# DeltaNet and quick-GELU FFN on one core: raw keys with norms in row scales, and 32x32 transposes to the lanes, for chunks 0 and 1

## The chip, the core and the metric

The kernel runs on one core of a Trainium2 chip. The metric is the device time of one execution in microseconds. Engines: TensorE (PE, with PEld for its weight loads), VectorE (DVE), ScalarE (ACT), GpSimd (POOL) and SyncE (SP, which here only issues DMAs). Each has its own instruction stream; semaphores tie them together. DMAs are issued by SP, POOL or ACT.

## What is computed

A delta-rule recurrence for 4 batches of 8 heads, 768 steps, head width 48, and behind it a feed-forward block on the 3072 x 384 rows that result.

```python
k_n = k / (np.linalg.norm(k, axis=-1, keepdims=True) + 1e-06)
for t in range(S):
    y[:, :, t] = np.einsum('bhd,bhde->bhe', q[:, :, t], state)
    v_old = np.einsum('bhde,bhd->bhe', state, kt)
    state = state + bt[:, :, :, None] * np.einsum('bhd,bhe->bhde', kt, vt - v_old)
...
h = x @ w_in                                  # (3072, 384) @ (384, 2048)
g = h * (1.0 / (1.0 + np.exp(-1.702 * h)))
return (g @ w_out)                            # (2048, 384)
```

`q`, `k`, `v`, `beta` are float32. `w_in` and `w_out` reach the core as 64-bit words and are turned into float32 there by integer operations.

## The kernel before

**Tiling.** The 768 steps are cut into 6 chunks of 128. A *unit* is one chunk of one batch with its 8 heads; units are numbered chunk by chunk, `n = 4c + b`, so units 0 to 3 are chunk 0 and 4 to 7 chunk 1. In a chunk the recurrence becomes a triangular system: with G the Gram matrix of the keys, the updates U solve (I + diag(beta) strict_lower(G)) U = diag(beta) (V - K S). It is solved by blocks of 32 rows: the four 32x32 diagonal blocks of each head are inverted, and then come four steps of "multiply by the inverse of the block" (`solve`, PSUM tile `psU`, copied to `US` by ACT) and "subtract from the rows below" (`below`, tile `psR`, subtracted from `V` by DVE).

**The inverses.** Four units have 4 x 8 x 4 = 128 diagonal blocks, one for each SBUF partition ("lane"). Tile `NT` holds them with the 32x32 block along the free dimension, and `invert` works on all 128 lanes at once on DVE: multiply by beta (`NT<-NT,bI`), 15 growing products and sums for the 16-halves, 10 more for the corner, and a last multiply by beta (`NT<-YB,bI`). Blocks come to the lanes through DRAM (`Nd<-TW` or `Nd<-G`, then `NT<-Nd`) and go back through DRAM (`Yd<-NT`, then `XB<-Yd`). For chunks 2 to 5 `invert` works on two units at a time.

**Preparing a unit.** The keys are normalised in place (in chunk 0 by `normalize_first`, in chunk 1 by `normalize_mixed`, later by `normalize`, with POOL), transposed on PE (`turn`: `psT`, copied to `kT` by ACT), and `gram` makes G (`psG`, copied by ACT). `Step.scores` transposes the queries and makes the masked scores `M` (`psQ`; POOL's affine_select cuts the triangle). `queries`, `outputs` and `state` make the output (`psY`, copied to `xT` and `last`; `last` is spread over `xT` by six small DMAs for each pair of units) and the new state `ST`.

**Feed-forward.** `hidden` multiplies by `w_in` (`ph`, activation on ACT into tiles `gT`); `both_written`, `written` and, from the third pair on, `seven` (Strassen-like, with combinations of weights that POOL makes once in `combined`, tiles `TW` and `w_out`) multiply by `w_out` (`po`).

**Weights.** `fetch_in(i)` brings a quarter of raw `w_in` in 12 DMAs, 6 on SP and 6 on SP or POOL; raw words share space with `w_out`, two quarters at a time, so quarter 2 can come only when quarter 0 is converted. `conversion` takes five DVE operations and one on ACT for a piece; `fill(n)` emits n steps of that stream, so the code places them by hand between the other work. `fetches` names which DMA may follow which converted piece.

**Order.** Operations are pinned to program order, but for some of POOL and SP in `woven`. They run: load keys, normalise, blocks to the lanes, grams, `invert(0)` (with scores of units 0 to 3 on PE and ACT), hops of units 0 and 1 (`hops`, `together`: one unit solves while the other subtracts), `put_out`, hops of units 2 and 3 with `hidden` of the first pair and the keys of chunk 1 in between, `invert(1)` with `hidden` of both pairs, then the loop `woven`, in which three neighbouring units are in flight and a queue of feed-forward work is spent in shares. `warm(n)` puts n throw-away matmuls (`ps_warm`) on PE.

Of the kernel before, what the change touches and what calls it, by code (L numbers as in the profile page):

```python
# [18 lines left out]
def kernel(  # L19
# [39 lines left out]
    NW, NA, NY, NU = 80, 3, 28, 4  # L59
# [21 lines left out]
    QP += [TW[:, a : a + H * DP].rearrange("p (h d) -> p h d", h=H) for a in (2048, 2560)]  # L81
    NT = cpool.tile([128, BS, BS], F32, name="NT")
# [63 lines left out]
    act.activation(table, ident[:, 0:1], ACT.Copy)  # L146
# [21 lines left out]
    def quarter(i):  # L168
        size = KC * NQ * 2
        return as_raw(raws[:, i % 2 * size : (i % 2 + 1) * size], (KC, NQ))  # L170
# [13 lines left out]
    outside = {0: "xT", 8: "xT", 11: "xT", 1: "M", 9: "M", 14: "M", 2: "M2", 10: "M2", 15: "M2"}  # L184
    order = [0, 1, 2, 3, 4, 5, 6, 7, 8, 13, 9, 10, 12, 11, 14, 15]

    def fetch_out(f):

        if f in outside:
            slot = outside[f]  # L190
            if slot not in slots:
                slots[slot] = wk.tile([128, 2 * DM], I32, tag=slot[:2].strip("2"), name="raw", bufs=3)
            words = slots[slot]
        else:
            words = raws[:, inside[f] * DM : (inside[f] + 2) * DM]
        places[f] = as_raw(words, (1, DM))
        sync(out=as_rows(places[f])[:, 0], in_=moe_w_out[f * 128 : (f + 1) * 128, :])
# [51 lines left out]
    def conversions():  # L249
# [28 lines left out]
        ("in", 1): lambda: fetch_in(2),  # L278
        ("in", 3): lambda: fetch_in(3),
# [32 lines left out]
    def normalize_mixed(n):  # L312
        K = KN[n % len(KN)][:, :, 0:D]
        ksq = wk.tile([128, H, D], F32, tag="ksq", name="ksq", bufs=1)
        act.activation(ksq, K, ACT.Square)
        yield
        ssq = wk.tile([128, H], F32, tag="ssq", name="ssq", bufs=4)
        vec.tensor_reduce(ssq, ksq, axis=AX.X, op=ALU.add)
        rn = wk.tile([128, H], F32, tag="rn", name="rn", bufs=4)
        pool.tensor_tensor(rn, ssq, half, op=ALU.pow)  # L320
        yield
        vec.tensor_scalar(rn, rn, 1e-6, None, op0=ALU.add)
        vec.reciprocal(rn, rn)
        vec.tensor_tensor(K, K, rn.broadcast_to([128, H, D]), op=ALU.mult)
        yield

    def normalize_first():
# [3 lines left out]
        z = wk.tile([128, 4, B, H], F32, tag="ksq", name="z", bufs=1)  # L331
        x, y, t, s = (z[:, i] for i in range(4))
        sq = spare("squares")[:, 0 : 2 * H * D].rearrange("p (o h d) -> p o h d", o=2, h=H)
        for b in range(B):
            act.activation(sq[:, b % 2], KN[b][:, :, 0:D], ACT.Square)
            vec.tensor_reduce(s[:, b], sq[:, b % 2], axis=AX.X, op=add)
        ts(x, s, 1e-30, None, op0=ALU.max)
# [5 lines left out]
        tt(s, s, y, op=mult)  # L343
        ts(s, s, 1e-6, None, op0=add)
        vec.reciprocal(s, s)
        for b in range(B):
            K = KN[b][:, :, 0:D]
            tt(K, K, s[:, b].broadcast_to([128, H, D]), op=mult)
# [35 lines left out]
    def prepare(n):  # L384
# [4 lines left out]
        G = gram(n)  # L389
        Nd = dram.tile([H * NS], F32, tag="Nd", name="Nd", bufs=4)  # L390
# [8 lines left out]
            out=NT[b * NB * H : (b + 1) * NB * H],  # L399
# [7 lines left out]
    def spare(name):  # L407
        at = {"M": 0, "blocks": 0, "QS": 1024, "squares": 1024, "U": 2048, "M5": 2048}[name]
        return TW[:, at:]

    def diagonal(b, D_):

        kT = kTs[b]
        ps = [ps_seq.tile([128, NP, 128], F32, tag="seq", name="psD") for _ in range(2)]
        for h in range(H):
            r = slice(h % 2 * 64, h % 2 * 64 + D)
            pe.matmul(
                ps[h % 2][:, h // 2], lhsT=kT[r, h // 2, :], rhs=kT[r, h // 2, :],
                start=True, stop=True,
            )  # L420
        for e in range(2):
            for blk in range(NB):
                u = slice(blk * BS, (blk + 1) * BS)
                copy = vec.tensor_copy if e == 0 or blk == 0 else act.copy
                copy(D_[u, e::2, :], ps[e][u, :, u])

    def invert(c, b0=0, nb=B):
# [4 lines left out]
        bc = bI[part, c].broadcast_to([np, BS, BS])  # L432
# [34 lines left out]
        act.activation(X1, halves(Y)[1].rearrange("p l i -> p i l"), ACT.Copy)  # L467
# [20 lines left out]
        if c == 0:  # L488
            warm(NY, vec.memset)
        YS = N  # L490
        vec.tensor_tensor(YS, Y, bc, op=ALU.mult)
        if c == 0:
            gate = wk.tile([128, 1], F32, tag="gate", name="gate", bufs=1)
            pool.tensor_copy(gate, YS[:, 0, 0:1])
        dma = sync if c < 3 else nc.sync.dma_start
        groups = [range(b0, b0 + nb)] if c > 0 else [range(HB), range(HB, B)]
        back = {}
        for bs in groups:
            for b in bs:
                back[b] = dram.tile([H * C, BS], F32, tag="Yd", name="Yd", bufs=4)  # L500
                (beside if c == 0 and b >= HB else dma)(
                    out=back[b].rearrange("(p j) i -> p j i", j=BS),
                    in_=YS[(b - b0) * NB * H : (b - b0 + 1) * NB * H],
                )
            for b in bs:
                XB = wk.tile([128, H, BS], F32, tag="XB", name="XB", bufs=4)
                dma(out=XB, in_=back[b].rearrange("(h t) i -> t h i", h=H))
                inverse[c * B + b] = XB
# [8 lines left out]
    class Step:  # L517
# [19 lines left out]
        def scores(self):  # L537
# [7 lines left out]
            if c > 0:  # L545
# [4 lines left out]
                spare("M" if self.n < B else "M5")[:, 0 : H * 128].rearrange("p (h t) -> p h t", h=H)  # L550
                if self.n in (B - 1, B + 1)
# [121 lines left out]

    def g_tile():

        return wk.tile([128, FQ, NTH], F32, tag="gT", name="gT", bufs=GB)

    def hidden(xT, gT, t, cost, sums=None, late=False):

        n = t.stop - t.start  # L680
        for f0 in range(0, FC, 2):
            if f0 // FQ == len(gT):
# [43 lines left out]

# [85 lines left out]

    def both_written(c, gT):

        po = [ps_moe.tile([128, DM], F32, tag="moe", name="po") for _ in range(HB)]
        for n, f in enumerate(order):
            while ("out", f - f % 2 if 4 <= f < 8 else f) not in done:
                fill(1)
            fill(3)
# [64 lines left out]
    def follow(n):  # L884
# [6 lines left out]
        if n - 1 + B < len(units):  # L891
# [63 lines left out]
    for blk in range(NB):  # L955
        sync(out=bI[blk::NB, 0], in_=betas[:, 0, blk, :])
# [5 lines left out]
    fetch_in(0, other_queue)  # L962
# [3 lines left out]
    pool.memset(half, 0.5)  # L966
    pool.memset(ST, 0.0)
    for U in US:
        pool.memset(U[:, H * D :], 0.0)
    for i in range(B, len(KN)):  # L970
        pool.memset(KN[i][:, :, D:DP], 0.0)


    warm(NW)
    normalize_first()
    Ds = spare("blocks")[:, 0 : B * H * BS].rearrange("p (b h j) -> p b h j", b=B, j=BS)
    Nds = []
    turn(0)
    for b in range(B):
        if b + 1 < B:  # L980
            turn(b + 1)
        diagonal(b, Ds[:, b])
        Nd = dram.tile([H * C * BS], F32, tag="Nd", name="Nd", bufs=4)
        sync(out=Nd.rearrange("(h p k) -> p h k", p=C, k=BS), in_=Ds[:, b])
        Nds.append(Nd)
    for b in range(B):
        sync(
            out=NT[b * NB * H : (b + 1) * NB * H].rearrange("d i k -> d (i k)"),
            in_=Nds[b].rearrange("(d r) -> d r", r=BS * BS),
        )  # L990
    for b in range(B):
        load(b, ((QP, q),), sync)
    for b in range(B):
        load_values(b, sync)
# [150 lines left out]
```

## Time and profile before

| | us |
|---|---|
| three timed runs | 815.26, 820.82, 827.23 (median 820.82) |
| the profiled execution | 815.16 |
| its span, first to last instruction | 813.5 |
| busy: PE / weight loads / DVE / ACT / POOL | 748.9 / 636.4 / 501.4 / 238.5 / 249.4 |

The page cuts the span into 40 slices of 20.3 us; a digit is a busy share in tenths, PEclk the granted TensorE clock in tenths of full speed.

```profile
PE   8678889777789779999999999999999999999998
DVE  5797581998578667668767777786676681110000
PEclk9576599889799989999999999999999999999999
DMA  9945466244112410420421323224204102000000
```

From the fifteenth slice or so on PE is full and its clock is whole. In the slices ahead of that, some 290 us, PE is not full, the clock is often below one, and DVE is full in places. Some stages of that part, by the trace:

| us | what runs |
|---|---|
| 0 to 30.7 | keys, norms, blocks of chunk 0 to the lanes |
| 30.7 to 58.4 | `invert(0)` on DVE |
| 58.4 to 63.0 | inverses back, by DRAM |
| 63.0 to 87 | hops and outputs of units 0 and 1 |
| 87 to 125 | hops and outputs of units 2 and 3, keys of chunk 1, raw w_in converted |
| 125 to 142.5 | blocks of chunk 1 to the lanes, by DRAM |
| 142.5 to 171.2 | `invert(1)` on DVE |
| 171.2 to 220.3 | raw w_out converted, first steps of `woven` |
| 220.3 to 290.3 | `woven`, POOL's combinations of weights (267.3 to 282.0) |
| 290.3 to 813.5 | `woven` with both halves of its work, and the tail |

### The profile page before, as it was taken

Reading aid. Unit: us, or ns where it says so; the run is one execution under the profiler, and the core shown is the slowest. Engines: PE = TensorE matmul, PEld = TensorE weight load, DVE = VectorE, ACT = ScalarE, POOL = GpSimd, SP = SyncE. Lnnn points to the kernel's source line nnn. Section 1 sums busy time; section 2 is a strip of 40 time slices with the busy share of each in tenths; the row PEclk is TensorE's granted clock in tenths of the full one; section 3 lists DMA queues with packets and bytes.
Section 4 is the critical chain, followed back from the end, with each engine's and each line's share of the span. In section 5 each row is a group of like instructions: output and inputs, shape, how many; then the busy total and the mean of one; then the engine's idle time right before and its main releaser. Section 6 shows DMA issues by size and latency. Waiting matters only on the chain.

```text
span 813.5 us, 19675 instructions
## 1 busy us (share of the span) xinstructions
PE 748.9 (92%) x8464; PEld 636.4 (78%) x8464; DVE 501.4 (62%) x1029; ACT 238.5 (29%) x523; POOL 249.4 (31%) x210
## 2 busy tenths in 40 slices
PE   8678889777789779999999999999999999999998
PEld 6566668644456669889888898898898898998988
DVE  5797581998578667668767777786676681110000
ACT  3332263223323322242232232332422312312120
POOL 5011030011023826235254262282160330502213
PEclk9576599889799989999999999999999999999999
DMA  9945466244112410420421323224204102000000
GB/s 163 148 74 106 102 173 163 43 111 118 55 50 66 102 45 18 103 63 18 106 53 42 83 54 74 58 56 103 56 18 94 21 15 47 2 25 2 22 3 19
DMA packets 143654, 54.45 MB, mean 67 GB/s; under 512 B 113664, under 2 KB 138368, under 8 KB 143568
## 3 DMA queue, kind: packets, MB, share of 16 engines
q1 hardware_dynamic: 141936, 48.42, 27.0%
q0 software_dynamic: 1536, 4.52, 2.3%
q8 instruction: 66, 1.08, 0.6%
q10 hardware_dynamic: 96, 0.26, 0.1%
q14 instruction: 20, 0.16, 0.1%
HBM read 33.13 MB, written 18.87 MB: 64 GB/s over the span
## 4 chain that ended last, share of the span: by engine, by line
PE 70%; DVE 16%; DMA 4%; POOL 3%; issue 3%; SPq 2%; ACT 1%; DVEq 0%; POOLq 0%
PE ph L109 25%; PE po L109 24%; PE psY L109 6%; PE psU L109 5%; DVE P L109 4%; PE psQ L109 3%; DVE YB L109 3%; PE psT L109 2%; DVE TW L109 2%; PE psG L109 2%; SPq L109 2%; PE psR L109 2%; DVE NT L109 2%; DVE w_out L109 2%; POOL TW L711 1%
## 5 line engine op out<-in xcount | busy, mean ns | idle before, releaser
L109 PE MATMUL ph<-xT,w_in 128*128 128x256 f32 x1152 | 268.7, 390 | 0.0
L109 PEld LDWEIGHTS ph<-xT,w_in 128*128 128x128 f32 x1152 | 219.8, 194 | 33.3 <-DVE V L109 1.4
L109 PE MATMUL po<-w_out,gT 128*128 128x192 f32 (+1 forms) x736 | 152.8, 361 | 18.7 <-DVE w_out L109 11.0
L109 PEld LDWEIGHTS po<-w_out,gT 128*128 128x128 f32 x736 | 122.3, 193 | 37.2 <-DVE w_out L109 14.8
L711 POOL TENSOR_TENSOR gT<-gT 128x512 f32<-128x512 f32 x80 | 105.8, 1331 | 124.6 <-ACT gT L109 114.1
L109 DVE TENSOR_TENSOR V<-V,psR 64x384 f32<-64x384 f32 (+1 forms) x96 | 53.3, 556 | 134.7 <-PE psR L109 133.5
L109 DVE TENSOR_TENSOR P<-NT,YB 64x2 f32<-64x2 f32 (+9 forms) x200 | 98.4, 492 | 6.4
L109 ACT ACTIVATE gT<-ph 128x512 f32<-128x512 f32 x92 | 54.9, 596 | 152.9 <-PE ph L109 152.8
L109 PEld LDWEIGHTS psU<-V,XB 32*32 32x32 f32 x1536 | 61.6, 109 | 31.5 <-issue 16.5
L109 DVE TENSOR_REDUCE YB<-P 64x2 f32<-64x2 f32 (+9 forms) x200 | 81.8, 409 | 6.9
L109 PE MATMUL po<-TW,gT 128*128 128x192 f32 x480 | 83.0, 328 | 0.0
L109 ACT COPY US<-psU 32x384 f32<-32x384 f32 x92 | 43.2, 469 | 125.0 <-PE psR L109 115.4
L109 PE MATMUL psU<-V,XB 32*32 32x48 f32 x1536 | 73.0, 209 | 6.5 <-DVE V L109 4.8
L109 PEld LDWEIGHTS po<-TW,gT 128*128 128x128 f32 x480 | 77.9, 190 | 1.1 <-issue 0.3
L109 PE MATMUL psR<-US,G 32*32 32x48 f32 x2208 | 63.1, 207 | 0.6 <-ACT US L109 0.5
L578 POOL TENSOR_SCALAR_AFFINE_SELECT M<-M 128x1024 f32<-128x1024 f32 x19 | 23.6, 1245 | 123.5 <-DVE M L109 62.1
L109 DVE TENSOR_TENSOR o<-o,po 128x192 f32<-128x192 f32 x40 | 13.5, 351 | 75.8 <-PE po L109 75.3
L109 PEld LDWEIGHTS psR<-US,G 32*32 32x32 f32 x2208 | 53.5, 108 | 2.0 <-ACT US L109 1.1
L94 POOL DMA_DIRECT2D KN<-in_k_dram x15 | 14.4, 959 | 99.0 <-PE psY L109 99.0
L109 DVE TENSOR_TENSOR P<-NT 64x512 f32<-64x512 f32 (+7 forms) x50 | 43.0, 860 | 2.1
L109 PE MATMUL ps_warm<-ident 128*128 128x256 bf16 x176 | 31.5, 339 | 11.4 <-ACT G L109 6.5
L109 PE MATMUL psQ<-QS,kT 48*128 48x176 f32 (+1 forms) x368 | 35.5, 337 | 4.9 <-ACT QS L109 4.8
(110 smaller groups left out, 776.8 us busy)
## 6 DMA issues: line engine op xcount, KB each, us to landing
Nd<-G SPq DMA_DIRECT2D x20, 512.0 KB, 3.5
V<-in_v_dram SPq DMA_DIRECT2D x24, 192.0 KB, 3.2
out_dram<-o SPq DMA_DIRECT2D x24, 192.0 KB, 2.6
QP<-in_q_dram SPq DMA_DIRECT2D x22, 192.0 KB, 3.4
w_out<-in_moe_w_in_dram SPq DMA_DIRECT2D x18, 192.0 KB, 4.6
raw<-in_moe_w_out_dram SPq DMA_DIRECT2D x9, 384.0 KB, 4.0
NT<-Nd SPq DMA_DIRECT2D x24, 128.0 KB, 2.6
XB<-Yd SPq DMA_DIRECT2D x24, 128.0 KB, 3.1
```

The costliest lines, as they stand in the source:

```text
L94: dma(out=place(dst, n)[:, :, 0:D], in_=src[b, :, c * C : (c + 1) * C, :].rearrange("h p d -> p h d"),)
L109: return lambda *a, **kw: tc.keep_in_program_order(op(*a, **kw))
L578: (pool if self.n < B else nc.gpsimd).affine_select(out=self.M, in_=self.M, compare_op=ALU.is_gt, fill=0.0, base=0, pattern=[[0, H], [1, 1 ...
L711: (engine or nc.gpsimd).tensor_tensor(o, a, b, op=op)
```

## The change

- Keys of chunks 0 and 1 are no longer scaled. They are transposed and multiplied raw. With l the length of a key, the system is solved for U/l: `lengths` makes l, turns it to the lanes by a 32x32 transpose (`across`) and puts beta / l^2 (`scale`) in place of beta in `invert`; `lengthen` multiplies the values by l. `normalize_first` and `normalize_mixed` go.
- Diagonal blocks of these chunks are made by 32x32 matmuls of their own (`diagonal`), two units in a pair of PSUM banks, copied by two operations, and go to the lanes and back by DVE transposes of 128x1024 (`lanes`, `tokens`). The DRAM trips of these two chunks go; chunks 2 to 5 keep theirs.
- The four units of chunk 0 hop in one loop, two pairs in turn; their outputs follow one after the other. The first pair's `hidden` and chunk 1's keys come behind that.
- Raw quarters 0 and 1 of `w_in` lie in `GT`, the space of the `gT` tiles, so that all four are fetched at the start; queries and values are loaded earlier too. `w_out` pieces 2, 10 and 15 come through `TW`.
- Warm matmuls are fewer: 80 to 14 at the start, 36 around the grams and scores of chunk 0 to none, 28 to 12 (and not held for DVE) before the hops, 4 to 2 in each hop. The activation table of the GELU is loaded at the start.
- 18 steps of w_out's conversion are put ahead of `invert(1)`, and `both_written` begins within it as far as pieces are converted.

```diff
-    NW, NA, NY, NU = 80, 3, 28, 4
+    NW, NA, NY, NU, NF = 14, 3, 12, 2, 18
...
+    def squares(n, sq):
+        act.activation(sq, KN[n % len(KN)][:, :, 0:D], ACT.Square)
+        vec.tensor_reduce(
+            sums_of[:, n % B * H : (n % B + 1) * H], sq, axis=AX.X, op=ALU.add
+        )
+
+    def lengths(c):
...
+        tt(length, sums_of, y, op=mult)
+        ts(length, length, 1e-6, None, op0=add)
+        vec.transpose(across, length)
+        vec.reciprocal(scale, across)
+        tt(scale, scale, scale, op=mult)
+        tt(scale, scale, bI[:, c], op=mult)
+
+    def lengthen(n):
+        V = loaded[n]
+        vec.tensor_tensor(
+            V, V, length[:, n % B * H : (n % B + 1) * H].broadcast_to([128, H, D]), op=ALU.mult
+        )
...
+    def lanes():
+        vec.transpose(
+            NT.rearrange("p i k -> p (i k)"), Ds.rearrange("p l k -> p k l")
+        )
+
+    def tokens(c):
+        vec.transpose(
+            XBs.rearrange("p l i -> p i l"), NT.rearrange("p j i -> p i j")
+        )
...
-        bc = bI[part, c].broadcast_to([np, BS, BS])
+        bc = (bI[part, c] if c > 1 else scale).broadcast_to([np, BS, BS])
...
-        act.activation(X1, halves(Y)[1].rearrange("p l i -> p i l"), ACT.Copy)
+        (vec.tensor_copy if c < 2 else act.copy)(X1, halves(Y)[1].rearrange("p l i -> p i l"))
...
+    warm(NW)
+    for n in range(B):
+        squares(n, sq[:, n % 2])
+        turn(n)
+        diagonal(n)
+        if n == 1:
+            keep_diagonals(n)
+    lengths(0)
+    keep_diagonals(B - 1)
+    lanes()
...
+    warm(NY)
...
+    paths = hops(*pair[:2]), hops(*pair[2:])
     for i in range(2 * NB):
-        together(*next(path))
-        warm(NU)
-        fill(1)
-    for s in pair[:2]:
+        for path in paths:
+            together(*next(path))
+            warm(NU)
+            fill(1)
+        if i % 2:
+            pair[i // 2].select()
+    for s in pair:
         put_out(s)
-        fill(1)
+        fill(2)
...
     while not ("in", 7) in done:
-        fill(1)
+        ahead_of(preparing, 1)
+        fill(2)
+        feed()
     run(preparing)
+    fill(NF)
+    both = both_written(0, gTs[0])
+    for n in range(B, 2 * B):
+        lengthen(n)
     inverting = invert(1)
     first = new_step(B)
-    for i in range(25):
+    for i in range(27):
         ahead_of(inverting, 1)
         feed()
+        if not ffn and i % 2:
+            next(both)
```

## The prediction

> **What bounds it now.** I read the page's slices first, then the windows cut at the stages of the program, then the chain that ended last, then VectorE's timeline at the places where that chain changes engine. The windows (us from the span's start; busy us of PE, weight loads, DVE, ACT, POOL; granted clock; DMA share; GB/s) say where PE is the limit and where not:
>
> ```profile
> 0.00:30.70 30.70, 23.08 (x191) 18.83 (x193) 18.13 (x53) 11.89 (x26) 10.98 (x33) 0.83 0.87 150
> 30.70:58.40 27.70, 21.24 (x161) 16.45 (x158) 25.83 (x54) 11.18 (x27) 0.00 (x0) 0.68 0.71 98
> ...
> 63.00:87.00 24.00, 22.16 (x434) 17.43 (x434) 15.84 (x22) 7.29 (x18) 1.49 (x1) 0.64 0.40 82
> ...
> 125.00:142.50 17.50, 17.50 (x93) 15.14 (x92) 1.57 (x2) 4.98 (x10) 0.55 (x1) 1.00 0.63 167
> 142.50:171.20 28.70, 22.42 (x99) 18.63 (x97) 26.87 (x57) 6.54 (x14) 1.09 (x1) 0.88 0.17 30
> 171.20:220.30 49.10, 35.86 (x311) 21.17 (x312) 40.80 (x84) 15.47 (x29) 8.64 (x7) 0.87 0.42 111
> ...
> 290.30:813.50 523.20, 515.80 (x5961) 462.02 (x5959) 288.43 (x603) 142.03 (x318) 182.04 (x139) 1.00 0.20 47
> ```
>
> From 290 us on, TensorE is busy 515.8 of 523.2 us at full clock. The instruction order there is unchanged, so I carry these 523.2 us over. All that the change can win lies before, where VectorE (25.8 of 27.7 us, 26.9 of 28.7, 40.8 of 49.1) and the DMA carry the chain:
>
> ```profile
> 24.61 2.14 DMA Nd<-TW
> 26.77 0.30 SPq L109
> 27.12 3.57 DMA QP<-in_q_dram
> 30.69 1.22 DVE NT L109
> ...
> 57.21 1.20 DVE NT L109
> 58.47 2.02 DMA Yd<-NT
> ```
> ```profile
> 132.35 7.60 DMA Nd<-G
> 139.97 2.56 DMA NT<-Nd
> 142.54 1.24 DVE NT L109
> ```
>
> The reader should see the two trips through DRAM: blocks to lanes (24.6 to 30.7 in chunk 0, 132.4 to 142.5 in chunk 1) and back (58.4 to 63.0, the first psU). Before chunk 1's solve VectorE stands:
>
> ```profile
> 142.54 1.23 DVE L109 TENSOR_TENSOR NT<-NT,bI 128x1024 f32<-128x1024 f32 x1 [15.94 <-DMA NT<-Nd]
> ```
>
> **Start to the first solve.** Before: norms, four key scalings (1.96 us), the psT/psD chain, 32 partial copies, two DMA legs; the solve starts at 30.7. After: keys are transposed raw as they land (ACT takes them at 3.87, 5.17, 6.45, 7.93). Per unit ACT has one square (0.52) and one kT copy (0.60), and psT takes 0.67. The last kT is out near 10.0, psD (0.7, as a 16-instruction psU group at full clock) near 10.8. VectorE's norm chain took 9.07 to 11.98; with a small transpose and two multiplies at 0.2 each and the reciprocal (0.35) it runs from 10.0 to 13.9, then one psD copy (0.5) and a 128x1024 transpose. No row shows a transpose: bounds are 0.9 (1024 elements at the rate of the fastest 768-element row, 0.69) and 4.46 (a 1024-element multiply, NT<-NT,bI at 274.2, stretched beside POOL); I take 1.25, because the nearest row is the undisturbed 1024-element multiply, 1.22. Solve starts at 15.7: 15.0 us won. Beta, now on the path, is queued just behind the keys on SP and has some 6 us of slack.
>
> **First solve to the first hop.** Same instructions, 27.7 us, plus the X1 copy on VectorE (0.42, a 128x256 copy), two value scalings (0.56 each) and the transpose back (1.25): 30.5, so the first psU is at 46.2 instead of 63.0. The lead is now 16.8. Grams, scores and selects of four units (8x0.55 + 4x0.60 + 16x0.3 = 11.6 us of ACT) hide under the solve. Queries and values are loaded earlier: SP issues four keys (2.73), four betas (2.88), four queries (3.35), six pieces of w_in (4.45) and then the values, near 14 to 20; by bytes keys 0.8, queries 0.8, first w_in quarter 1.6 and values 0.8 MB at the slices' 150 GB/s are in at 27 us, before the 42 where values are scaled. All four raw quarters and three more keys make 9.2 MB, 61 us; the last quarter is converted after 90. So the early w_in costs nothing; without that cover it would cost what the trace shows at 102 us, where VectorE stands 5.09 us for raw w_in, a stall that goes. Queued behind 24 POOL issues (0.54 each, six took 3.23) is now the memset of the late U, and ACT's fourth US copy waits for that: the last issue waits for the 16th piece to land, 2.1 MB, which at half of 150 GB/s takes 28 us from 7, so 35, against 47 when needed. At a quarter of the rate it would be 63: bounds 0 and 16 us; I take 0, by the two queues' equal shares of w_in.
>
> **Hops of four units.** 16 groups alternate between two pairs. VectorE needs 16 subtractions at 0.56 and 16 conversion steps, about 14 of 0.9 us of them waiting for nothing: 21.4. A group on PE at half clock is 16 steps at 0.079 plus two warm matmuls (0.97/2): 1.8 to 1.85, so 29.6; at full clock VectorE's 21.4 binds. PE idles some 20 us before, as the 12 warms are no longer held for the solve's end. I take 27, to 73.
>
> The clock, row first: granted 0.50 from 24 us; though PE was fed from 28.5, it came back to 1.00 only near 46, and it fell to 0.5 again from 68 to 84 while small matmuls ran. The Trainium skill (TensorE: Matmul & The Clock Gate, part 1) speaks against cutting warms: an idle window of about 3.4 us halves the clock, but by it one busy window restores it. By the rule the hops would take about 23 us and the total would be 4 lower; the row shows a slower return, so the row decides.
>
> **Put-outs, keys of chunk 1.** Four put-outs of 16+16 psY at half clock (4.68 a pair): 9.4, to 82. The change adds a wait: `last` is one buffer, so ACT's copy for the third unit waits for six xT DMAs (SP issue 4.6, landing 1.8). Queued behind it on ACT are a conversion step and the next square, for which VectorE waits: 89 before it goes on, 6 of them idle. Then 16 w_in steps (0.9) and reduces, with ACT per unit 3.7 us (square, kT, two G, relu, gelu): 18 us, to 107. Then norms 3.9, two psD copies, two steps and the transpose: 114.6. The G round trip (10.1 us and 15.9 of idle VectorE) is gone. Next are 18 w_out steps (0.48): 123, and four value scalings: 125.5. Second solve: 28.7 + 0.4 + 1.25, to 155.7 against 171.2. DMA in that stretch: keys 0.8, queries 0.4, values 0.8 and eight raw pieces of w_out at 0.39, 5.1 MB from 76 on at the 158 to 226 GB/s of the windows; raw w_out lands some 5 us ahead of its conversion.
>
> **After the second solve.** 52 of the 70 w_out steps are left against 69; 17 x 0.5 = 8.5 us shorter, since this stretch is VectorE's (40.8 of 49.1 busy): 40.6. Then 47.0 as before. The four POOL combinations (3.45+3.43+3.40+4.30, then psT after 7.86 us of idle PE) come one po group earlier in POOL's order; the key scaling behind the first waits 3.4, the rest leave earlier: gain 0 to 6, I take 4.
>
> **Sum.** 16.8 + 0.2 (46.2 to 125.5 against 63.0 to 142.5) - 1.5 + 8.5 + 4 = 28 us. The profiled execution took 815.2 (813.5 plus 1.7 around it): 787. It was the fastest of those shown; the median is 5.7 above. Halfway, I predict 790.
>
> **Rivals.** (1) VectorE alone binds between first psU and second solve: its work there is 9.0 + 36 + 1.4 + 2.2 + 3.9 + 2.2 + 8.6 + 2.3 = 66 instead of my 79, gain 41, so 774 profiled and about 777. For it: full clock in hops and SP early enough with xT. Against: 0.5 clock in both old hop stretches. (2) The tail of the prologue does not shorten: conversions still wait for raw w_out, which now shares the DMA with keys, queries and values, and POOL's combinations stall as before. Then 28 - 8.5 - 4 = 15.5 remain: 800, about 803. For it: 226 GB/s at 172 to 180, a full queue. Transposes at the upper bound (4 x 3.2 = 13) land there too. (3) The clock stays at half until the second solve's end: after psD at 114, 69 hidden matmuls remain (two passes of 0.22 each, 30.3), psT and psQ 2, po 6.5: 38.8 against 41 until the solve is over. So it begins to cost below a mean clock of 0.95. At 0.5 it costs 36 here, 3 in the hops and 8 in the key loop (psT, two ph groups, psG: 3.1 a unit becomes 6.1, 24.6 for four against 18, and psD): 47 - 28 = 19 slower, 834, about 837. The gain is gone where 38.8 grows by 17 beside the other 11, at a mean clock of 0.7. Against: dense hidden matmuls had 1.00 from 112 to 156. (4) The change doesn't do what it says: a wait on beta, values or the late U puts the solve or hops back by 6 to 10: 795 to 798.
>
> **Chances.** Forecast 0.53 (own range 781 to 798), rival 1 0.18, rival 2 0.19, rival 3 0.05, rival 4 0.05. The range takes in rival 1 down to 772 and rival 2 to 808. Two per cent, about what a measurement here tells from no change, is 804.4: faster 0.53 + 0.18 + 0.05 + 0.09 of rival 2 = 0.85; same 0.11 with the rest of rival 2 and a milder rival 3; slower 0.04.
>
> **What would show it.** NT's first multiply near 16 us with no DMA before it; first psU near 46; clock near 0.5 in the hops; some 6 us of idle VectorE at the third put-out; the second NT multiply near 125 with no DMA wait; psT after the combinations near 261. I am wrong if a transpose takes over 3 us, if ACT or PE ends the wait before V in chunk 1, or if the part from that psT on is not 523 us long.

## The result, and the profile after

The changed kernel took 813.73 us (median of 19 runs, 810.43 to 815.83); the kernel before took 820.44 in the same job (19 runs, 811.83 to 827.23). The ratio is 0.9935, 95% interval 0.9915 to 0.9955: 0.65% faster, where 3.7% was forecast, and outside the range. The profiled execution of the changed kernel spans 812.0 us, so its own time is at the median; the one of before, with 813.5 us, was among the fastest of its kernel. The two traces therefore differ by 1.5 us where the medians differ by 6.7: where the other 5 us of the kernel before arise, no trace here shows.

The windows of the changed kernel, cut at its own stages (us from the start; busy us of PE, weight loads, DVE, ACT, POOL; granted clock; DMA share; GB/s):

```profile
0.00:20.50 20.50, 11.78 (x305) 9.18 (x306) 9.01 (x28) 6.81 (x14) 14.03 (x39) 0.82 1.10 155
20.50:53.40 32.90, 21.90 (x140) 17.84 (x139) 31.06 (x57) 12.11 (x28) 7.46 (x11) 0.50 1.08 180
53.40:84.90 31.50, 31.50 (x672) 23.14 (x672) 23.57 (x34) 11.09 (x20) 0.00 (x0) 0.50 0.07 12
84.90:99.50 14.60, 10.78 (x139) 9.32 (x138) 7.65 (x13) 5.21 (x17) 1.83 (x2) 0.73 0.29 63
99.50:124.80 25.30, 23.01 (x383) 18.65 (x384) 20.68 (x41) 12.56 (x24) 0.83 (x1) 0.89 0.69 174
124.80:136.50 11.70, 4.16 (x19) 3.31 (x18) 11.46 (x23) 3.75 (x6) 0.00 (x0) 0.83 0.36 108
136.50:174.00 37.50, 33.35 (x152) 27.04 (x150) 29.52 (x60) 7.95 (x16) 1.09 (x1) 0.96 0.03 6
```

The rows are: start, first solve, hops, put-outs, key loop, w_out steps, second solve. The trips through DRAM are gone: the first multiply on NT waits for no DMA any more (its line is below, at 136.55). But in the hops TensorE is busy all the time (31.50 of 31.50 us), in the w_out steps TensorE works 4.16 of 11.70 us, and in the second solve it works 33.35 of 37.50 where it had 22.42 of 28.70 before.

Where the lead arises and where it ends is read from the timelines of the engines. "Solve" is the first multiply on NT, "psQ n" the first score matmul of unit n; e1 to e18 are the experiments below.

| kernel | solve 1 | first psU | solve 2 | psQ 6 | psQ 7 | psQ 8 | psQ 9 | median us |
|---|---|---|---|---|---|---|---|---|
| before | 30.7 | 63.0 | 142.5 | 225.6 | 247.6 | 267.2 | 307.6 | 820.4 |
| changed | 20.5 | 53.4 | 136.6 | 224.4 | 247.9 | 274.2 | 305.8 | 813.7 |
| forecast | 15.7 | 46.2 | 125.5 | | | | | 790 |
| e1 | 20.9 | 53.7 | 128.9 | 218.0 | 241.6 | 264.4 | 304.4 | 811.7 |
| e2 | 20.9 | 53.7 | 142.3 | 227.5 | 251.1 | 277.4 | 309.4 | 817.6 |
| e3 | 20.3 | 53.1 | 134.6 | 212.6 | 235.0 | 261.0 | 292.9 | 801.5 |
| e4 | 20.4 | 53.2 | 135.4 | 223.9 | 247.3 | 273.6 | 305.2 | 813.0 |
| e5 | 20.5 | 53.4 | 134.5 | 222.6 | 246.1 | 272.4 | 304.0 | 813.4 |
| e6 | 20.2 | 58.5 | 139.9 | 227.4 | 250.8 | 277.1 | 310.6 | 821.0 |
| e7 | 17.0 | 52.1 | 134.8 | 222.4 | 245.9 | 272.2 | 303.8 | 813.0 |
| e9 | 20.4 | 53.2 | 130.4 | 218.4 | 245.1 | 271.3 | 303.0 | 811.5 |
| e10 | 21.0 | 53.8 | 136.4 | 224.2 | 247.6 | 268.8 | 301.7 | 819.9 |
| e11 | 20.9 | 53.8 | 137.1 | 225.2 | 248.6 | 269.8 | 306.3 | 814.1 |
| e12 | 18.7 | 53.9 | 130.9 | 218.3 | 245.0 | 271.1 | 302.9 | 806.5 |
| e13 | 20.4 | 53.3 | 128.1 | 215.6 | 237.0 | 263.6 | 296.1 | 805.1 |
| e14 | 17.8 | 51.3 | 127.3 | 216.0 | 239.7 | 266.1 | 297.6 | 802.9 |
| e15 | 18.0 | 50.4 | 124.7 | 213.4 | 235.0 | 261.6 | 294.1 | 801.7 |
| e17 | 20.6 | 53.5 | 136.4 | 224.1 | 245.5 | 272.1 | 304.6 | 812.4 |
| e18 | 29.6 | 62.2 | 144.8 | 227.4 | 248.8 | 268.5 | 305.4 | 809.5 |

A lead of 10.2 us at the first solve is 9.6 at the first psU, 6.0 at the second solve, 1.2 at psQ 6 and 1.8 at psQ 9; from there to the end both kernels need the same (506.1 and 505.9 us). e5 has the changed kernel's instructions in the same order (why is told below), and its second solve came 2.0 earlier: differences of 2 us between two profiles mean nothing, and the medians decide.

The lines that answer to the wait on NT of before are, on PE and then on DVE:

```profile
135.80 4.57 PE L111 MATMUL ph<-xT,w_in 128*128 128x256 f32 x12 [7.54 <-ACT GT L111]
```
```profile
136.55 1.22 DVE L111 TENSOR_TENSOR NT<-NT,small 128x1024 f32<-128x1024 f32 x1
...
159.77 0.42 DVE L111 TENSOR_TENSOR V<-V,psQ 128x96 f32<-128x96 f32 x2 [6.05 <-PE psQ L111]
```

VectorE no longer stands 15.94 us before the second solve. But during that wait TensorE had been busy 17.50 of 17.50 us with the hidden layer, which now lies elsewhere: when the second solve began, 115 of its 192 matmul records had started before the change, and 74 after it. What is left runs inside the solve, and V waits 6.05 us for psQ, which stands behind it.

### The profile page after: what moved, and what is told of

It reads as the page before. It is cut to its first block, busy times and chain, and to the rows that moved or that the text cites. A ratio compares the mean times of both kernels' runs of the same rounds, so it can differ in the third digit from the quotient of the medians.

```text
span 812.0 us, 20270 instructions
## 1 busy us (share of the span) xinstructions
PE 747.4 (92%) x8794; PEld 633.9 (78%) x8794; DVE 505.5 (62%) x1030; ACT 234.5 (29%) x512; POOL 245.9 (30%) x217
## 3 DMA queue, kind: packets, MB, share of 16 engines
q8 instruction: 69, 1.13, 0.6%
## 4 chain that ended last, share of the span: by engine, by line
PE 78%; DVE 15%; issue 3%; ACT 2%; DMA 1%; POOL 0%; SPq 0%; DVEq 0%; POOLq 0%; ACTq 0%
PE ph L111 30%; PE po L111 25%; PE psU L111 7%; PE psY L111 5%; DVE P L111 4%; PE psQ L111 4%; DVE YB L111 2%; PE psT L111 2%; PE psR L111 2%; DVE NT L111 2%; PE psG L111 2%; DVE w_out L111 2%; PE ps_warm L111 1%; DMA xT<-last 1%; DVE TW L111 1%
## 5 line engine op out<-in xcount | busy, mean ns | idle before, releaser
L111 PE MATMUL po<-w_out,GT 128*128 128x192 f32 (+1 forms) x736 | 155.4, 365 | 16.1 <-DVE w_out L111 12.4
L111 PEld LDWEIGHTS po<-w_out,GT 128*128 128x128 f32 x736 | 123.9, 195 | 36.0 <-DVE w_out L111 16.5
L736 POOL TENSOR_TENSOR GT<-GT 128x512 f32<-128x512 f32 x80 | 105.9, 1332 | 122.8 <-ACT GT L111 112.2
L111 DVE TENSOR_TENSOR V<-V,psR 64x384 f32<-64x384 f32 (+1 forms) x96 | 53.3, 556 | 138.9 <-PE psR L111 137.7
L111 ACT ACTIVATE GT<-ph 128x512 f32<-128x512 f32 x92 | 54.8, 596 | 153.5 <-PE ph L111 153.4
L111 PEld LDWEIGHTS psU<-V,XB 32*32 32x32 f32 x1536 | 67.6, 116 | 39.4 <-issue 31.4
L111 PE MATMUL psU<-V,XB 32*32 32x48 f32 x1536 | 79.1, 217 | 11.0 <-DVE XB L111 11.0
L111 PE MATMUL po<-TW,GT 128*128 128x192 f32 x480 | 83.0, 328 | 0.0
L111 PEld LDWEIGHTS po<-TW,GT 128*128 128x128 f32 x480 | 77.9, 190 | 1.1 <-issue 0.3
L111 DVE TENSOR_TENSOR P<-NT 64x512 f32<-64x512 f32 (+7 forms) x50 | 48.8, 976 | 1.9
L308 POOL TENSOR_TENSOR rn<-ssq,half 128x8 f32<-128x8 f32 x16 | 35.0, 2186 | 12.8 <-DVE ssq L111 12.8
```

The costliest lines, as they stand in the source:

```text
L111: return lambda *a, **kw: tc.keep_in_program_order(op(*a, **kw))
L308: nc.gpsimd.tensor_tensor(rn, ssq, half, op=ALU.pow)
L736: (engine or nc.gpsimd).tensor_tensor(o, a, b, op=op)
```

## The experiments

Unless another is named, an edit is to the changed kernel. Times are medians, compared with the kernel before on the same chip.

**The w_out steps and the hidden layer.**

e1:
```diff
-    NW, NA, NY, NU, NF = 14, 3, 12, 2, 18
+    NW, NA, NY, NU, NF = 14, 3, 12, 2, 0
```


> None of the 18 w_out steps is put ahead of the second solve; they follow it. Theory A (the lead is lost because the GELUs of the hidden layer stand behind these steps on ScalarE, so that TensorE waits 7.5 us and VectorE later 6.0 us at V): the second solve starts 8 us earlier, near 128, TensorE has no wait of over 2 us before it, the hidden layer is done before V needs psQ, and of the 8.7 us of steps put behind the solve some hide under the po matmuls; total 806 to 810. Theory B (VectorE binds from the put-outs to the fifth group and the steps cost the same wherever they stand): the start is 8 us earlier, the stretch after the solve 8.7 us longer, total 812 to 816.

e2:
```diff
-    fill(NF)
+    for _ in range(NF):
+        fill(1)
+        feed()
```


> The 18 w_out steps stay ahead of the second solve, but a step of the hidden layer is issued after each. Theory A (order on ScalarE): TensorE's 7.5 us at GT goes, the hidden layer is done some 15 us earlier, VectorE's 6.0 us at V goes and the first po matmuls run beside the solve; total 6 to 8 us less than the changed kernel, 805 to 808. Theory B (VectorE binds): the waits go but TensorE stands later at w_out instead; total 811 to 814.

e3:
```diff
-                for j in range(KC):
+                for j in range(1 if sums is None else KC):
```


> Left out: two of the three matmuls of each group of the hidden layer for chunk 0 (64 of 96 passes, 0.22 us each, 14 us of TensorE), so part of the output is another. Theory A (after the change TensorE's own work beside the second solve binds, as the trip through DRAM that covered it is gone): VectorE's wait of 6.05 us at V goes and total falls by 8 to 14 us, to 800 to 806. Theory B (VectorE and the order of its steps bind): total falls by at most 3, to 811 to 814.

e1 took 811.67 us (0.9916, 0.9877 to 0.9955). The second solve came 7.6 us earlier and TensorE's 7.54 us at GT were gone, so the GELUs had indeed been behind the conversion's relus on ScalarE (its one step for a piece; four of them ran between the GELUs at 118.6 and 135.2 us); but po then waited 10.6 us for w_out, and of 6.4 us of lead on the changed kernel at psQ 6, 1.4 was left at psQ 9. e2 took 817.61 us (0.9992, 0.9956 to 1.0029), slower than the changed kernel and outside both theories: both named waits went, but the conversions now waited for relus behind GELUs (solve 5.7 us later), and po matmuls put ahead of psQ waited 14.6 us for w_out. These are the largest PE waits of e2 (us, times, longest):

```profile
PE po L111 <- DVE w_out L111: 23.6, 7, 14.6
PE ph L111 <- DMA xT<-last: 3.6, 1, 3.6
```

e3 took 801.46 us (0.9806, 0.9748 to 0.9865), 12 us below the changed kernel, as theory A said, but its expectation had undercounted what it left out: 128 of 192 records, and TensorE was busy 26.4 us less (721.02 against 747.43 up to 810 us). Some half of that work lay on the chain. So neither order of the w_out steps that was tried helps; TensorE's matmuls between the put-outs and psQ, which the DRAM trips had covered, bind much of that stretch.

**The third put-out, and the hops.**

e4:
```diff
-                lasts[0] = wk.tile([128, NTH], F32, tag="last", name="last", bufs=1)
+                lasts[0] = (
+                    wk.tile([128, DM], F32, tag="o", name="o")[:, 0:NTH] if self.n == HB
+                    else wk.tile([128, NTH], F32, tag="last", name="last", bufs=1)
+                )
```


> The second pair of units gets a `last` of its own (an o tile that is unused then), so the third put-out waits for no DMA. Theory A (this wait is on the path): VectorE's idle 8 us between 85 and 100 goes, the key loop and the second solve come 6 to 8 us earlier, total 806 to 809. Theory B (TensorE at half clock or a later wait takes it up): the key loop starts earlier but the second solve comes at most 2 earlier; total 812 to 815.

813.04 us (0.9936, 0.9903 to 0.9969). The first reduce of the key loop came 2.8 us earlier (96.72 instead of 99.48), the second solve 1.2, which is within the scatter: the wait is there, as forecast, and costs next to nothing. Theory B.

e6:
```diff
-    warm(NY)
+    warm(28, vec.memset)
...
-            warm(NU)
+            warm(4)
```


> The warm matmuls as before the change: 28, held for the end of the first solve, and 4 instead of 2 after every group of the hops. Theory A (TensorE runs the hops at the slow pace, 276 ns a psU matmul and 31.5 us for 16 groups, because it stood idle from 45 to 53 us): the matmuls go at 0.20 to 0.23 us, the hops take 24 to 26, the key loop starts 6 us earlier and the total is 806 to 810. Theory B (the hops are slow in any case, or what they gain is taken up by the wait for `last` and by TensorE's work later): hops above 29, or total 812 to 816.

e9:
```diff
-            warm(NU)
```


> No warm matmuls in the hops (32 of 0.41 us, 13.0 us of TensorE's 31.6). Theory A (the hops are TensorE's: slow, and the warm matmuls are nearly half of them, so they cost and keep nothing warm): the hops take 21 to 25 us, the second solve starts 6 to 9 us earlier, at 128 to 131; the total goes down by less, to 807 to 811, since TensorE's work behind the solve is near its bound. Theory B (the hops hang on the round between TensorE, ScalarE and VectorE): hops above 28 and total 812 to 815.

e6 took 820.97 us (1.0043, 1.0007 to 1.0078): the held matmuls put the first psU 5.1 us back, and the hops took 31.7 us (58.49 to 90.19), as long as in the changed kernel, since 64 warm matmuls at a median of 0.34 us filled what the psU and psR matmuls saved (medians of 0.25 and 0.20 instead of 0.276 us). e9 took 811.54 us (0.9931, 0.9899 to 0.9963): hops of 25.4 us (53.23 to 78.66). The warm matmuls of the changed kernel's hops, on PE (count, duration in ns min/median/max, first and last start), and then one group of its hops (a pair of them, the first psU behind it, the next pair):

```profile
L111 PE MATMUL ps_warm<-ident x32: 393/406/421, 54.8 to 84.6; 128*128 128x256 bf16 x32
```
```profile
58.70 0.61 PE L111 MATMUL ps_warm<-ident 128*128 128x256 bf16 x2
59.24 0.28 PE L111 MATMUL psU<-V,XB 32*32 32x48 f32 x1
...
60.67 0.61 PE L111 MATMUL ps_warm<-ident 128*128 128x256 bf16 x2
```

The durations of the 32 add up to 13.0 us, but those of a pair overlap: a pair takes 0.54 us of a group's 1.97, 8.6 us in 16 groups, and the hops without them were 6.1 us shorter. They kept nothing warm: the psU matmuls have a median of 0.276 us with them and without them. The second solve came 6.1 us earlier and psQ 6 as well, and then half of it was lost between psQ 6 and psQ 7. That place is taken up below.

**The start.**

e7:
```diff
-    fetch_in(0, other_queue)
...
-    fetch_in(3, other_queue)
...
+    act.copy(GT[:, 0:1], kTs[B - 1][:, 0, 0:1])
+    fetch_in(0, other_queue)
...
+    fetch_in(3, other_queue)
     lanes()
```


> The transfers of raw w_in (and the values and keys queued behind them) wait until kT of the fourth unit is out, so the DMA rings are nearly empty while the first diagonals are computed. Theory A (TensorE's 2.6 to 4.5 us of 'issue' in the middle of the fourth unit's transposes is its instructions coming late through the DMA that the early w_in fills): the stall is under 1 us, the first solve starts near 16 instead of 20.4, the first psU is near 49; total 808 to 812. Theory B (it comes from the 256 small psD matmuls whatever the DMA does): the stall stays above 2.5 us and the solve starts at 20 or later; total 813 to 816.

e16:
```diff
-            NT.rearrange("p i k -> p (i k)"), Ds.rearrange("p l k -> p k l")
+            NT.rearrange("p i k -> p (i k)"), Ds.rearrange("p l k -> p (l k)")
```


> Changed: the transposes into lanes read the blocks in the order in which they lie, head outside and column inside, not column outside with a stride of 32, so that the lanes hold other numbers. Theory A (the stride makes a 128x1024 transpose cost 1.95 us): it takes 1.0 to 1.3 us. Theory B (a transpose of 1024 elements costs that whatever its order): 1.9 to 2.0 us. The total moves by at most 1 us.

Where TensorE stands in the transposes of the fourth unit, in the changed kernel, the wait in brackets:

```profile
15.99 0.37 PE L111 MATMUL psT<-ident,KN 128*128 128x128 f32 x1 [4.51 <-issue]
```

and in e7:

```profile
12.38 0.27 PE L111 MATMUL psT<-ident,KN 128*128 128x128 f32 x1 [1.48 <-issue]
```

The stall, which waits for nothing that the profile shows, is 2.63 to 4.98 us in the fourteen profiles with the early w_in and 0.33 to 1.48 in the four in which w_in comes behind the fourth kT (e7, e12, e14, e15); the fourth kT is out at 13.3 instead of 17.0 in e7. That most of it goes with the early loads (w_in and what is queued behind it) is shown; that it is TensorE's instructions that come late is argued only. The total did not move (813.0 us; 0.9969, 0.9935 to 1.0002): of 3.5 us at the solve 1.3 were left at the first psU. Where they went, on DVE in e7:

```profile
37.12 0.42 DVE L111 TENSOR_REDUCE YB<-P 128x64 f32<-128x256 f32 x1
37.45 5.21 DVE L111 TENSOR_TENSOR V<-V,small 128x384 f32<-128x384 f32 x2
```

and on POOL in e7:

```profile
36.84 1.14 POOL L111 DMA_DIRECT2D w_out<-in_moe_w_in_dram  x2 [1.36 <-DMA w_out<-in_moe_w_in_dram]
37.96 0.13 POOL L111 MEMSET TW<- 128x16 f32 x1
38.02 3.18 POOL L111 TENSOR_SCALAR_AFFINE_SELECT M<-M 128x1024 f32<-128x1024 f32 x3
41.15 1.09 POOL L111 TENSOR_SCALAR_AFFINE_SELECT TW<-TW 128x1024 f32<-128x1024 f32 x1
```

The four selects had queued up behind POOL's DMA issues; they ran as one block, and two scalings of V, 1.02 us in the changed kernel, took 5.21 and ended 0.4 us behind it. In e16 the transposes into the lanes took 1.25 us at 18.82 and at 124.29, instead of 1.95 and 1.97; the ones back, whose input was still strided, 2.01:

```profile
18.82 1.25 DVE L111 STREAM_TRANSPOSE NT<-TW 128x1024 f32<-128x1024 f32 x1
50.58 2.01 DVE L111 STREAM_TRANSPOSE XB<-NT 128x1024 f32<-128x1024 f32 x1
```

So the stride makes the difference (one run, 813.28 us).

e12 has the edits of e4, e7 and e9; e14 adds
```diff
-    fetch_in(2, other_queue)
-    fetch_in(3, other_queue)
+    fetch_in(2)
+    fetch_in(3)
```


> Three edits together: no warm matmuls in the hops, the raw w_in behind the fourth kT, a second `last`. Theory A (what is won ahead of the second solve stays as far as TensorE's remaining work allows): second solve near 124 to 127, 10 to 12 us ahead of the changed kernel, total 804 to 808. Theory B (TensorE's matmuls from the put-outs to the steady part bind and it only waits elsewhere): second solve early as above, but total 810 or more.

> As the run with three edits, and the raw pieces of the last two quarters of w_in are issued by SyncE alone, so GpSimd's memset and four selects are not queued behind twelve more of its DMA issues. Theory A (the first solve kept only 1.3 of the 3.5 us because the selects, held up, ran as one block of 4.3 us from 38 us on, beside which two V scalings took 5.2 us instead of 1.0): the selects run from 22 to 37 us, the two scalings take about 1 us, the first psU comes near 50 to 51 instead of 53.9 and the second solve 3 us earlier, total 804 to 807. Theory B (SyncE's longer queue holds something else up): first psU at 53 or later, total 808 or more.

e12 took 806.54 us (0.9884, 0.9843 to 0.9926), but its first psU and second solve are those of e9: the same block of selects, at 39.29 to 43.5. In e14 the selects run from 26.3 to 37.8 us, each when its M is there, the two scalings take 1.02 again, the first psU comes at 51.3 and the second solve at 127.3: 802.92 us (0.9814, 0.9763 to 0.9866).

**The four combinations on GpSimd.** e5 lets `between(hidden(...))` emit one combination after every fourth step of the next hidden layer; e8 is e5 with e1's edit; e10 emits them through the pinned engine; e11 only moves them to VectorE. First e5's edit (`combined` there returns its four operations instead of emitting them), then e11's:

```diff
-        combined()
+        combos.extend(combined())
...
+    def between(work):
+
+        for i, cost in enumerate(work):
+            if combos and i % 4 == 3:
+                combos.pop(0)()
+            yield cost
+        while combos:
+            combos.pop(0)()
...
-            queue.append(hidden(xTs[h], gT, slice(0, NTH), 1.3, sums))
+            queue.append(between(hidden(xTs[h], gT, slice(0, NTH), 1.3, sums)))
```
```diff
-            add(o, a, b, sub_)
+            add(o, a, b, sub_, vec)
```


> The four combinations of w_out on GpSimd no longer go in one burst after the last group of the first layer, but one after every fourth step of the next hidden layer. Theory A (the burst keeps the key scaling of later units waiting on GpSimd, and VectorE's operations beside it take 3 to 4 us in place of 0.2 to 1.0, so whatever lead there is ends here): no 3.2, 4.1 and 2.8 us operations on VectorE in a row, the wait of psT for KN (5.1 us) goes, psQ of the eighth unit comes 7 to 9 us earlier than 274.2 and the total is 803 to 807. Theory B (the four stalls only move): VectorE is stretched by the same 3.3 us four times later on, TensorE waits there, total 811 to 815.

> No w_out steps ahead of the second solve and the combinations spread, both. Theory A: the run without these steps was 6.4 us ahead of the changed kernel at psQ of the sixth and seventh units and lost it in the 40 us from the eighth to the ninth, where the combinations are; with these spread the lead stays: psQ of the ninth unit near 296 instead of 304 to 306, total 801 to 805. Theory B (TensorE's work before the steady part is what binds): no more than the spread alone gives, within 2 us of that run.

> The combinations spread over the next hidden layer, now in an order that is kept (in the two kernels before, the scheduler put them back in one burst: their instructions stood as in the kernels without the edit). Theory A (the burst of 14 us on GpSimd, with VectorE stretched beside it and KN's scaling behind it, takes the lead): psQ of the eighth unit at 264 to 267 instead of 272 to 274, total 803 to 807. Theory B (spread or not, each of the four holds VectorE for 3.4 us, and TensorE comes to wait for VectorE or KN there): total 810 to 815.

> The combinations on VectorE (1536 elements, an estimated 1.8 us each from the 1.22 us of 1024 elements) instead of GpSimd (3.4 to 3.7). Theory A: 7.3 us of VectorE in place of 14 us of GpSimd with 9 us of stretched VectorE operations beside it; KN's scaling is not held up; total 807 to 810. Theory B (VectorE's queue is as full there): 811 to 815.

e5 and e8 tested nothing: GpSimd's unpinned operations are ordered by the scheduler, which put the four back where they were. They serve as repeats, 813.38 us against 813.73 and 811.47 against 811.67. In the changed kernel the burst and VectorE beside it look so, POOL first:

```profile
255.81 3.42 POOL L736 TENSOR_TENSOR TW<-w_out 128x1536 f32<-128x1536 f32 x1 [2.09 <-PE po L111]
259.63 1.09 POOL L312 TENSOR_TENSOR KN<-KN,rn 128x384 f32<-128x384 f32 x1 [0.41 <-DVE rn L111]
260.69 3.42 POOL L736 TENSOR_TENSOR w_out<-w_out 128x1536 f32<-128x1536 f32 x1
264.54 7.47 POOL L736 TENSOR_TENSOR TW<-w_out,TW 128x1536 f32<-128x1536 f32 x2 [0.43 <-PE po L111]
```
```profile
256.02 3.23 DVE L111 TENSOR_SCALAR rn<-rn 128x8 f32<-128x8 f32 x1
...
260.78 4.14 DVE L111 TENSOR_TENSOR P<-NT 64x768 f32<-64x768 f32 x1
264.96 0.94 DVE L111 TENSOR_REDUCE YB<-P 64x64 f32<-64x768 f32 x1
265.94 2.79 DVE L111 TENSOR_TENSOR P<-NT 64x448 f32<-64x448 f32 x1
```

An operation on 8 elements a lane takes 3.23 us and ends at 259.25, when GpSimd's subtraction ends at 259.23. The reduce at 264.96, beside another of them, takes its usual 0.94. Spreading the four (e10) made psQ 8 come 5.4 us earlier and psQ 9 4.1, but the last two combinations, at 300.5 and 307.1 us, then stood ahead of a KN scaling at 318.1 for which psT waited 6.07 us: the next psQ came at 337.5 instead of 333.6, and the total was 819.91 us (1.0018, 0.9983 to 1.0053). On VectorE (e11) psQ 8 came 4.4 earlier and psQ 9 no earlier: 814.13 us (0.9964, 0.9934 to 0.9993). The burst stretches VectorE, as theory A said, but neither way of breaking it up pays.

**psT's wait for KN.** In e9, on PE, between psQ 6 and psQ 7:

```profile
229.60 1.12 PE L111 MATMUL psT<-ident,KN 128*128 128x128 f32 x4 [3.38 <-POOL KN L312]
230.51 2.77 PE L111 MATMUL po<-w_out,TW 128*128 128x384 f32 x4
234.64 1.13 PE L111 MATMUL psY<-QS,ST 48*64 48x128 f32 x16
235.71 1.97 PE L111 MATMUL psY<-M,US 128*64 128x128 f32 x16
```

KN's scaling on GpSimd needs rn, and VectorE's two short operations on rn stood behind ten steps of the solve and a V subtraction. The next edit (e13 on e9, e15 on e14, e17 on the changed kernel, e18 on the kernel before) moves them up:

```diff
-        ahead_of(inverting, ahead[0])
+        if n % HB == 1 and n > B:
+            ahead_of(inverting, 5)
+            next(K, None)
+            ahead_of(inverting, ahead[0] - 5)
+        else:
+            ahead_of(inverting, ahead[0])
```


> Without warm matmuls in the hops, and in the odd units VectorE's two small operations on rn stand after five steps of the solve instead of after ten and the V subtraction. Theory A (the run without warm matmuls lost 3.1 of its 6 us between psQ of units 6 and 7, because psT waited 3.38 us for KN, whose scaling on GpSimd waits for rn on VectorE, and after that idle stretch TensorE's psY and psG groups took 1.13, 1.97 and 1.44 in place of 0.67, 1.09 and 1.16): the wait is under 2 us, the groups keep the short times, psQ of unit 7 is near 241.5 and the total 806 to 809. Theory B (the 3 us are lost to the order of other work): the wait shrinks, the total stays at 811 or more.

> The four edits of the run before and the early rn. Theory A (each removes a wait of its own on one chain): second solve near 127, psQ of unit 7 near 238, total 800 to 805. Theory B (TensorE's work from the put-outs on binds, so what comes earlier waits later): no more than 2 us better than the better of the two runs it is made of.

> The changed kernel with the early rn alone. Theory A (psT's waits for KN between psQ of units 6 and 9, 8.0 us in two, are a price of their own that lies behind whatever is won before): total 804 to 808, as far below the changed kernel as the early rn was below the run without warm matmuls (6 us). Theory B (the early rn pays only with a second solve that starts earlier): total 811 to 814.

> The kernel before the change with the early rn alone: it has the same waits for KN, 12.8 us in three. Theory A (the gain of the early rn is not the change's): 3 to 7 us faster than before, 811 to 815, so that the change is worth as little on top of it as without it. Theory B (before, VectorE is later there and takes no profit): within 2 us of before, so that change and early rn need each other.

e13, PE, the same place:

```profile
223.25 0.62 PE L111 MATMUL psT<-ident,KN 128*128 128x128 f32 x4
223.71 1.46 PE L111 MATMUL po<-w_out,TW 128*128 128x384 f32 x4
227.08 0.67 PE L111 MATMUL psY<-QS,ST 48*64 48x128 f32 x16
227.68 1.09 PE L111 MATMUL psY<-M,US 128*64 128x128 f32 x16
```

The wait is gone and the groups keep their short times: 805.14 us (0.9854, 0.9803 to 0.9905), 6.4 below e9. Theory A, with a part of the 8.1 us at psQ 7 due to a second solve that came 2.4 earlier without a reason in the code. e15 took 801.74 us (0.9800, 0.9751 to 0.9849; 6 runs, 797.71 to 804.63), the fastest. That lies in theory A's range too, but it is only 1.2 below e14, as theory B had it. On the changed kernel alone the early rn gave 1.3 us (e17: 812.41; 0.9924, 0.9893 to 0.9956), theory B; on the kernel before it gave 9.1 (e18: 809.51; 0.9887, 0.9839 to 0.9935), more than theory A's 3 to 7. The waits of PE from 225 to 310 us, before and in e18:

```profile
PE psT L109 <- POOL KN L309: 12.8, 3, 7.9
```
```profile
PE psT L109 <- POOL KN L309: 7.3, 2, 5.3
```

So with the early rn the kernel without the change (809.51) and with it (812.41) cannot be told apart in the change's favour: the intervals overlap, and the change has the slower median. What it won depends on orders that stand outside it.

## Why the prediction was wrong, point by point

All durations are of the two profiles. Forecast 785.3 us of span, measured 812.0; the 26.7 us between them fall on these steps.

- **"The early w_in costs nothing"** failed. I looked for its price on VectorE and on the queues of SP and POOL; it was paid on TensorE, 4.5 us of "issue" among the transposes, of which e7 took 3.0 away. With the next point it makes the first psU late by 7.2.
- **"I take 1.25" for a transpose**: mis-sized, 1.95 to 2.02, because the input is strided (e16: 1.25 without). Two lie before the first psU, 1.4 us, and in the solve VectorE was stretched beside the four selects by some 1.7, which I had priced at nothing.
- **"I take 27" for the hops**: 31.5, beyond my bound of 29.6. The 27 lay between VectorE's 21.4 and TensorE's 29.6 at half clock, but the pace was slow from the first group to the last. The price of a group at that pace was a little low too, 1.8 to 1.85 where it took 1.97: the 16 steps took 1.43 instead of 1.26, and the two warm matmuls 0.54 instead of half of 0.97, the time of four in the kernel before. e9 shows 25.4 without them. The half clock itself I had right (in the kernel before it began near 20 us already, not at 24), and rival 1 (VectorE alone binds) is out.
- **The third put-out**: the wait for `last` came, with ScalarE standing 5.01 us for it and VectorE behind ScalarE 3.98 instead of 6, but e4 shows that removing it gives about 1 us. The stretch took 14.6 us against 16.
- **Key loop and w_out steps**: 25.3 and 11.7 us by the windows, 37.0 together, against 25.6 and 10.9, together 36.5. Right. The second solve was therefore late by 11.0 for reasons that lay before them.
- **"38.8 against 41 until the solve is over"**: failed, 7.2 us. I let TensorE's hidden matmuls run from psD (the matmuls of the diagonal blocks) on, beside the 18 w_out steps. They stood, since their GELUs are behind the conversions on ScalarE (7.54 us), and 118 of 192 records were left for the solve. So PE ended the wait before V in chunk 1, the sign that I had named for being wrong. Of the 7.2 us, 6.05 are this wait. I had held TensorE's 38.8 us of work against the stretch as a whole, and asked neither whether it could run from its start nor where in it psQ stands. That TensorE had worked all through the 15.9 us which I listed as won was in the windows that I quoted (17.50 of 17.50).
- **"17 x 0.5 = 8.5 us shorter"**: the conversions did end sooner, 41.2 us after the solve (forecast 40.6, before 49.1). But from there to psQ 9 it took 90.7 us; I had 83.3, before 87.3. TensorE was behind, with the units' groups and po still to do: it was busy for 79.5 of these us (73.6 before) and waited for KN (8.0) and G (3.1) in the rest. This and **the combinations, "I take 4"**, cost 7.4 together: psQ 6 to psQ 9 took 81.4 us against 82.0 before, a gain of 0.6. The combinations came earlier, as forecast, and rn came under them, so psT still waited 5.1 us for KN and another 3.1 for G.
- **The steady part** is the same, as forecast. So is the place of the profiled execution: I put half of 5.7 us on top of the sum; the changed kernel's profile was at its median and the profile of before 5 us below its own.

Of the rivals, 2 named the place (the tail does not pay) but not the reason, since the conversions did end sooner; and 4 had a size near the 7.2 us by which the first psU was late, but the waits that it named (beta, values, the late U) did not occur. What the forecast lacked was a rival for TensorE's work losing its cover at full clock; I had tied that to the clock only. What stays open: how much of the last 7.4 us is the burst on GpSimd and how much TensorE's backlog. e3, with 26 us of TensorE work left out, had gained 11.8 us by psQ 6 and 12.9 by psQ 9; e10 and e11 changed the burst and gained nothing in the total.

## What to carry to other kernels

A wait that is removed was cover for other engines: before counting it as won, list what each of them did in it and where that work goes. A lead at the start of a prologue is worth only what the last wait of the prologue lets through, so look first for the cheap orders there (two short operations behind a long solve, here), with and without the change. Matmuls that are to keep TensorE warm are dropped where they keep nothing warm, as in these hops.

## What the runs showed of the hardware

- **GpSimd holds up some of VectorE's operations and not others.** An 8-element operation took 3.23 us beside a GpSimd subtraction of 3.42 and two scalings 5.21 beside 4.3 us of selects, while reduces beside GpSimd's operations were not stretched (0.94 us at 264.96 above). The Trainium skill (SBUF — State Buffer, "SBUF: two separate sides") describes a port pair that the two engines lock for a whole instruction; the rows of the stretched operations agree.
- **The same idle time of TensorE does not always cost the same.** After 2.98 us (changed kernel), 3.37 (e14) and 3.38 (e9) of waiting, psT took 1.11 to 1.12 instead of 0.62 (0.66 after 2.99 in the kernel before); in the first two psY was at 0.67 again some 4 us later, in e9 it was at 1.13 and stayed slow for 10 us. The granted clock says the same: 0.50 in 235 to 238 us, in 227 to 229.9 and in 229 to 239, and 1.00 in 233 to 245 of the kernel before. The Trainium skill (TensorE: Matmul & The Clock Gate, Part 1) has an idle window of about 3.4 us that runs freely; by where the window falls, one such wait could cost and another not, though all four are a little shorter than it. It also has one busy window restore the clock, and that the rows contradict: through 31.5 us of hops with TensorE busy all the time by the profile the granted clock was 0.50 and a psU matmul took 276 ns.
- **The granted clock can miss it.** In e1 the windows give 1.00 for 53 to 85 us and in the changed kernel 0.50, with the same work in the same time and psU matmuls of 276 ns in both; the matmuls' durations are the safer reading. First e1, then the changed kernel:

```profile
53.00:85.00 32.00, 31.31 (x672) 23.13 (x672) 24.26 (x35) 10.91 (x20) 0.00 (x0) 1.00 0.09 17
```
```profile
53.00:85.00 32.00, 31.61 (x674) 23.27 (x676) 23.97 (x35) 11.15 (x20) 0.00 (x0) 0.50 0.08 15
```
